# The second layer's weights split without GpSimd, and both parts of the last batch's work taken together

## The chip, the cores and the metric

The kernel runs on one core of one Trainium2 chip. The metric is the device time of one execution in microseconds (us); the time of before is a median of 3 runs. A profile records one execution, engine by engine: TensorE (PE, with its weight loads as PEld), VectorE (DVE), ScalarE (ACT), GpSimd (POOL) and SyncE (SP), whose queue issues most DMAs.

## The reference

Three layers one behind the other: an attention between 512 positions and 32 states for each of 8 batches and 8 heads, a dense layer, and a layer of 8 experts in which each token goes to one expert.

```python
scores = scale * np.matmul(x, state.transpose(0, 1, 3, 2))   # softmax, then a @ state
scores2 = scale * np.matmul(state, x.transpose(0, 1, 3, 2))  # softmax, then a2 @ x
x = np.concatenate([xread, sread], axis=2)                   # 8 x 544 tokens, 512 wide
...
h = x @ w_in                                                 # 512 -> 2048
g = np.maximum(0.01 * h, h)
x = g @ w_out                                                # 2048 -> 512
...
e_idx = np.argmax(x @ w_gate, axis=1)                        # 8 experts
for e in range(E):
    h = np.maximum(x[mask] @ w1[e], 0.0)                     # 512 -> 1024
    ye = h @ w2[e]                                           # 1024 -> 512
    out[mask] = gate_w[mask, None] * eom[mask, e, None] * ye
```

All inputs are fp32. The change is in the preparation of `w1` and `w2`, 8 experts with 4 MB together for each.

## The kernel before

PE multiplies numbers that are split in two parts, a high and a low one, with three products for each product of the reference. The dense layer uses two fp32r parts, the expert layer two fp16 parts. So the expert weights have to be split before that layer begins, and this runs beside the dense layer.

**The main loop** (from line 917) runs over steps `n`. A step is one block of 128 of the 2048 hidden columns (`f`, 0 to 15) of one chunk `c`; chunks 0 to 7 are the batches, chunk 8 holds the states' tokens. So step `n` is chunk `n // 16`, block `n % 16`. In a step, `mm1(n)` makes the hidden block `h` on PE (for two steps at a time behind a `kps` product), ACT and DVE make `u` from it (the leaky ReLU), then its parts `gh` (ACT) and `gl` (DVE), and `mm2(n - 2)`, two steps behind, adds the block before to four banks `y`. `gl` of a step is written at the start of the next one. `kl` is the low part of the other factor of `mm1`. The attention of the next batch runs beside it, up to the sixth chunk. At a chunk's end the four `y` are copied, their squares summed (ACT) and the **router** started, in pieces that `pump()` takes, one a step: split each row block in two fp16 halves (`halves`, lines 111 and 112), transpose them by DMA (`turn`, `yT`), logits on PE (`pl`, `lg`), choice, places (`pr`), scatter by POOL.

**The weight work** is the generator `presplit` (its loop from line 633), 32 jobs of two halves of 128 x 1024 fp32 each. `advance(pre)` takes it one of four parts on:

1. store the second half of the job before, load, sum the squares of the first half (ACT, `squares`, line 97);
2. the squares of the second half;
3. sum over the partitions (`tot`, two small products on PE, line 139), a power of two as scale from it (the norm: lines 647, 103, 104, 106 on DVE), then `halve` the first half;
4. store the first half, load, `halve` the second.

`halve` makes the fp16 high part `pc[:, 0]` on DVE (line 627), scales the fp32 tile in place on DVE (line 628), and subtracts on POOL for the low part (line 629). Of the 64 halves 14 belong to the last batch.

One part is taken in each step from step 14 on (line 957); in the last batch (`c` is 7, `f` from 2) a second one behind `mm2` and the pump (line 987). There parts 1 and 2 fall in even steps and 3 and 4 in odd ones, so a job takes two steps. In step 124 the states' result is split for chunk 8 (`srl`, line 933), at its start.

The order within an engine is the order in which the program is written: nothing is reordered, and an instruction that waits holds up all that stand behind it on its engine or queue.

Of the kernel before, what the change touches and what calls it, by code (L numbers as in the profile page):

```python
# [15 lines left out]
ALU = mybir.AluOpType  # L16
# [7 lines left out]
def tile_attention_moe_moe2(ctx, tc, x, state, w_in, w_out, w_gate, w_ogate, w1, w2, out):  # L24
    nc = tc.nc
    B, H, S, D = x.shape
# [54 lines left out]
                                   op=ALU.arith_shift_right)  # L81
    nc.vector.tensor_copy(tqf, tq)
    for t in range(NSR // 128):
        nc.vector.scalar_tensor_tensor(out=toks[:, t:t + 1], in0=tqf, scalar=float(TB - NS),
                                       in1=pidx_f, op0=ALU.mult, op1=ALU.add)
# [7 lines left out]
    def squares(o, t):  # L93

        k, n = t.shape[1:]
        with nc.allow_low_precision(reason="of the sum only the exponent is used"):
            nc.scalar.activation(out=junk[:, 0:k * n].rearrange("p (k n) -> p k n", n=n), in_=t, func=ACTF.Square,
                                 scale=2.0 ** 0.5, accum_out=o)
# [10 lines left out]
    def parts16(h, l, t, s):  # L109

        nc.vector.tensor_scalar(out=h, in0=t, scalar1=s, scalar2=None, op0=ALU.mult)
        nc.vector.scalar_tensor_tensor(out=l, in0=t, scalar=s, in1=h, op0=ALU.mult, op1=ALU.subtract)
# [22 lines left out]
    def over_partitions(*cols):  # L135

        ps = psa.tile([128, cols[0].shape[1]], FP32, tag="a", name="tot")
        for i, t in enumerate(cols):
            nc.tensor.matmul(ps, ones16.bitcast(BF16), t, start=(i == 0), stop=(i == len(cols) - 1))
        return ps  # L140
# [235 lines left out]
    def advance(g):  # L376
        try:
            next(g)
            return True
        except StopIteration:  # L380
            return False
# [210 lines left out]
    def presplit():  # L592

        jobs = [(e, half, m) for e in range(E) for half in range(2) for m in range(2)]

        SPARE = (NF * (B - 1) - NF + 2) // 4 + 1
        spare = {}

        def load(n, i):
            if n >= len(jobs) or (n, i) in spare:  # L600
                return spare.pop((n, i), None)
            e, half, m = jobs[n]
            k = (n - SPARE + 1) % 3 if n >= SPARE else 0
            shape = [128, KD, F2 // 4] if m == 0 else [128, KF // 4, DM]
            if k == 0:
                t = ps_p.tile(shape, FP32, tag="raw", name="raw")
            else:
                if i == 0:
                    room = x_p.tile([128, R, H, D], FP32, tag="x", name="x") if k == 1 else \
                        at1.tile([128, HP, R, 128], FP32, tag="xT", name="xT")  # L610
                    spare[n] = room.rearrange("p a b c -> p (a b c)").rearrange("p (i k f) -> p i k f", i=2, k=shape[1])
                t = spare[n][:, i]
            q = slice((2 * half + i) * 256, (2 * half + i + 1) * 256)
            if m == 0:
                nc.sync.dma_start(t, w1[e, :, q].rearrange("(k p) f -> p k f", p=128))
            else:
                nc.sync.dma_start(t, w2[e, q].rearrange("(k p) d -> p k d", p=128))
            return t

        def ahead(n):  # L620
            if n < len(jobs):
                t = load(n, 0), load(n, 1)
                spare[n, 0], spare[n, 1] = t

        def halve(t, s):
            pc = pq_p.tile([128, 2] + list(t.shape[1:]), FP16, tag="pc", name="pc")
            nc.vector.tensor_scalar(out=pc[:, 0], in0=t, scalar1=s, scalar2=None, op0=ALU.mult)
            nc.vector.tensor_scalar(out=t, in0=t, scalar1=s, scalar2=None, op0=ALU.mult)
            nc.gpsimd.tensor_tensor(out=pc[:, 1], in0=t, in1=pc[:, 0], op=ALU.subtract)  # L629
            return pc  # L630

        t0, last = load(0, 0), None
        for n, (e, half, m) in enumerate(jobs):
            wd = w1d if m == 0 else w2d
            if last is not None:
                nc.sync.dma_start(*last)
            t1 = load(n, 1)
            if n >= SPARE:
                ahead(n + 2)
            ss = sm.tile([128, 2], BF16, tag="ss2w", name="ss2w")  # L640
            squares(ss[:, 0:1], t0)
            yield
            squares(ss[:, 1:2], t1)
            yield
            sa = sm.tile([128, 1], FP32, tag="saw", name="saw")
            s = esc[:, m, half, e:e + 1]
            nc.vector.tensor_scalar(out=sa, in0=over_partitions(ss[:, 0:1], ss[:, 1:2]), scalar1=128.0, scalar2=2.0 ** -94,
                                    op0=ALU.mult, op1=ALU.max)
            norm_scale(sm, sa, s, einv[:, m, half, e:e + 1])
            pc = halve(t0, s)  # L650
            if n == SPARE - 1:
                ahead(n + 1)
                ahead(n + 2)
            yield
            nc.sync.dma_start(wd[e, :, 2 * half], pc)
            t0 = load(n + 1, 0)
            last = wd[e, :, 2 * half + 1], halve(t1, s)
            yield
        nc.sync.dma_start(*last)
# [23 lines left out]
    pre = presplit()  # L683
# [233 lines left out]
    for n in range(len(steps) + DEPTH):  # L917
        if n < len(steps):
            c, f = steps[n][0], steps[n][1]
            if f == 0:  # L920
                if attn_gen[0] is not None:
                    drain(attn_gen[0])
                    attn_gen[0] = None
                if c == 0:
                    attn_gen[0] = first_chunk()
                elif c + 1 < B:
                    attn_gen[0] = attention(c + 1)
            if c == B - 1 and f == 12:
                for i in range(2):
                    th = at.tile([128, 2, NSR], FP32R, tag=f"a1h{i}", name="srh")  # L930
                    tl = at.tile([128, 2, NSR], FP32R, tag=f"a1l{i}", name="srl")
                    nc.scalar.copy(out=th, in_=srT[:, 2 * i:2 * i + 2])
                    nc.vector.tensor_tensor(out=tl, in0=srT[:, 2 * i:2 * i + 2], in1=th.bitcast(FP32), op=ALU.subtract)
                    srh += [th[:, 0], th[:, 1]]
                    srl += [tl[:, 0], tl[:, 1]]
            if lo_part is not None:
                lo_part()
            hi_part = mm1(n)
            if c == B and f > 2:
                pump()  # L940
        conv = convert(n + 4, n + 1) if n + 1 < NF else convert()
        advance(conv)
        attend()
        if n < len(steps):
            lo_part = hi_part()
        elif lo_part is not None:
            lo_part()
            lo_part = None
        if n == 2:
            load_gates()  # L950
        if n == NF - 4:
            gate_squares()
        if n == NF - 3:
            gate_weights()
        drain(conv)
        if n + 2 >= NF:
            advance(pre)
        if n == NF * B:
            drain(pre)
            weight_scales()  # L960
            room.append([x_p.tile([128, R * H * D], FP32, tag="x", name="room"), 0])
            room.append(carve(E, E))
            nc.gpsimd.memset(room[1], 1.0)
            nc.gpsimd.affine_select(out=room[1], in_=room[1], pattern=[[1, E], [-1, E]], compare_op=ALU.is_ge,
                                    fill=0.0, base=0, channel_multiplier=0)
        if n == len(steps) - 3:
            w32_stack.close()
            wp = ctx.enter_context(tc.tile_pool(name="wp", bufs=1, side="right"))
            while active:
                pump()  # L970
            slot_regs(0)
            for q in range(4):
                w1t.append(wp.tile([128, 2, KD, F2 // 4], FP16, name=f"w1t{q}"))
                load_w(w1t, w1d, 0, q)
            for q in range(4):
                w2t.append(wp.tile([128, 2, KF // 4, DM], FP16, name=f"w2t{q}"))
                load_w(w2t, w2d, 0, q)
            for b in range(2):
                gather(b, r_p.tile([128, 2 * ROW], FP16, tag=f"row{b + 2}", name="row", bufs=1))
        if n == len(steps) + DEPTH - 1:  # L980
            transp(0, r_p.tile([128, 2 * KD, 128], FP16, tag="y", name="xt"))
        if n >= DEPTH:
            mm2(n - DEPTH)
        if n < 4:
            attend()
        pump()
        if c == B - 1 and f >= 2:
            advance(pre)
    ab.close()


# [96 lines left out]
```

## Time and profile before

| | |
|---|---|
| median of 3 runs (lowest, highest) | 1241.1 us (1239.32, 1241.99) |
| profiled execution, time | 1242.63 us |
| profiled execution, span of its trace | 1240.9 us |
| mean granted clock of PE | 0.977 of full speed |
| busy: PE, DVE, ACT, POOL | 95%, 64%, 39%, 31% of the span |
| line 629, POOL, 128 x 1024 (64 of them) | 152.00 us in all |

The busy share of an engine is an average over stages with different limits. What a change is worth has to be read in each stage from the engine that waits there and from what it waits for. Times within the trace are in us from the start of its span, which is 1.7 us shorter than the time of the execution.

### The profile page before, as it was taken

How to read it: one execution, taken by the hardware profiler on the slowest of the kernel's cores; microseconds unless marked ns; L12 is line 12 of the kernel's file. 1: busy time of each engine (PE TensorE's matmuls, PEld its weight loads, DVE VectorE, ACT ScalarE, POOL GpSimd, SP SyncE). 2: the span in 40 equal slices, each digit the busy share in tenths (PEclk: the TensorE clock that was granted, in tenths of full speed). 3: DMA queues.
4: the chain of work that ended last, by engine and by line, in shares of the span. 5: the costliest groups of instructions: out<-in, count | busy, mean ns of one | idle time of the engine just before them, and what ended most of it. 6: DMA issues, size and time to landing. Idle time of an engine off the chain costs nothing. (4 is left out here: it accounts for less than half of the span.)

```text
span 1240.9 us, 24399 instructions
## 1 busy us (share of the span) xinstructions
PE 1173.9 (95%) x9366; PEld 874.0 (70%) x9366; DVE 788.4 (64%) x1631; ACT 486.6 (39%) x950; POOL 380.4 (31%) x290
## 2 busy tenths in 40 slices
PE   5889999999999999999998887999999999999995
PEld 3557677777777777777776666877777777777773
DVE  6998786786786776786777888744643333333332
ACT  4876644544544545535444444321111111111111
POOL 3877224233323233232242353121211111111110
PEclk9899999999999999999998989999999999999998
DMA  5745346335445535445346732164216611133410
GB/s 164 223 154 136 107 119 170 99 111 170 132 119 146 154 106 165 112 129 151 95 145 187 212 135 87 52 204 166 74 52 240 260 53 44 44 128 111 182 50 23
DMA packets 133129, 161.65 MB, mean 130 GB/s; under 512 B 80015, under 2 KB 96399, under 8 KB 133008
## 3 DMA queue, kind: packets, MB, share of 16 engines
q1 hardware_dynamic: 124128, 131.65, 35.5%
q0 software_dynamic: 8880, 28.40, 6.6%
q8 instruction: 75, 1.23, 0.4%
q14 instruction: 46, 0.38, 0.1%
HBM read 229.71 MB, written 52.20 MB: 227 GB/s over the span
## 5 line engine op out<-in xcount | busy, mean ns | idle before, releaser
L739 PE MATMUL y<-woh,gh 128*128 128x512 f32 x544 | 227.7, 419 | 0.0
L741 PE MATMUL y<-woh,gl 128*128 128x512 f32 x544 | 217.3, 399 | 0.9 <-DVE gl L198 0.9
L740 PE MATMUL y<-wol,gh 128*128 128x512 f32 x544 | 217.0, 399 | 0.0
L629 POOL TENSOR_TENSOR pc<-raw,pc 128x1024 f16<-128x1024 f32 x54 | 128.0, 2370 | 248.7 <-issue 178.0
L1012 PE MATMUL h<-xt,w1t 128*128 128x128 f16 x1184 | 201.3, 220 | 0.0
L1013 PE MATMUL h<-xt,w1t 128*128 128x128 f16 x1184 | 201.2, 220 | 0.0
L1014 PE MATMUL h<-xt,w1t 128*128 128x128 f16 x1184 | 201.2, 219 | 0.0
L722 DVE TENSOR_TENSOR u<-h,u 128x512 f32<-128x512 f32 (+1 forms) x144 | 94.5, 657 | 114.7 <-ACT u L721 114.6
L1018 ACT ACTIVATE r<-h,room 128x512 f32<-128x512 f32 x74 | 50.8, 687 | 258.0 <-PE h L1014 258.0
L1020 DVE TENSOR_SCALAR rh<-h,room 128x512 f16<-128x512 f32 x74 | 55.5, 750 | 125.4 <-ACT r L1018 125.3
L1047 POOL DMA_INDIRECT out_dram<-osb,ti x37 | 37.5, 1014 | 310.9 <-DVE ti L1045 301.7
L197 ACT CAST gh<-u 128x512 fp32r<-128x512 f32 (+1 forms) x144 | 85.5, 594 | 109.0 <-DVE u L722 108.8
L739 PEld LDWEIGHTS y<-woh,gh 128*128 128x128 f32 x544 | 105.1, 193 | 31.9 <-issue 12.7
L741 PEld LDWEIGHTS y<-woh,gl 128*128 128x128 f32 x544 | 104.8, 193 | 25.6 <-DVE gl L198 1.3
L1012 PEld LDWEIGHTS <-w1t 128*128 128x128 f16 x1184 | 116.2, 98 | 4.7 <-issue 0.5
L1013 PEld LDWEIGHTS <-w1t 128*128 128x128 f16 x1184 | 116.2, 98 | 4.1
L740 PEld LDWEIGHTS y<-wol,gh 128*128 128x128 f32 x544 | 105.4, 194 | 18.8
L721 ACT ACTIVATE u<-h 128x512 f32<-128x512 f32 (+1 forms) x144 | 82.3, 572 | 88.4 <-PE h L717 86.9
L198 DVE TENSOR_TENSOR gl<-u,gh 128x512 fp32r<-128x512 f32 (+1 forms) x144 | 108.6, 754 | 12.1 <-ACT gh L197 10.3
L1014 PEld LDWEIGHTS <-w1t 128*128 128x128 f16 x1184 | 116.2, 98 | 0.0
L1037 PE MATMUL o<-w2t,rl 128*128 128x512 f16 x296 | 112.2, 379 | 0.1
L1035 PE MATMUL o<-w2t,rh 128*128 128x512 f16 x296 | 112.2, 379 | 0.1
(221 smaller groups left out, 2216.6 us busy)
## 6 DMA issues: line engine op xcount, KB each, us to landing
w1t<-w1s SPq DMA_DIRECT2D x152, 512.0 KB
w2t<-w2s SPq DMA_DIRECT2D x152, 512.0 KB
raw<-in_moe_w_dram SPq DMA_DIRECT2D x54, 512.0 KB
w1s<-pc SPq DMA_DIRECT2D x32, 512.0 KB
w2s<-pc SPq DMA_DIRECT2D x32, 512.0 KB
x<-in_x_dram SPq DMA_DIRECT2D x32, 256.0 KB
wir<-in_moe_w_in_dram SPq DMA_DIRECT2D x16, 512.0 KB
wor<-in_moe_w_out_dram SPq DMA_DIRECT2D x16, 512.0 KB
```

What stands on the lines that cost most here:

```text
L197: nc.scalar.copy(out=h, in_=t)
L198: return lambda: nc.vector.tensor_tensor(out=l, in0=t, in1=h.bitcast(FP32), op=ALU.subtract)
L629: nc.gpsimd.tensor_tensor(out=pc[:, 1], in0=t, in1=pc[:, 0], op=ALU.subtract)
L722: nc.vector.tensor_tensor(out=u, in0=ps, in1=u, op=ALU.max)
L739: nc.tensor.matmul(ys[c][t], gh[:, sl], woh[f], start=(f == 0), stop=False)
L740: nc.tensor.matmul(ys[c][t], gh[:, sl], wol[f], start=False, stop=False)
L741: nc.tensor.matmul(ys[c][t], gl[:, sl], woh[f], start=False, stop=(f == NF - 1))
L1012: nc.tensor.matmul(ps[:, i, :], wh, xt[:, k, :], start=(k == 0), stop=False)
L1013: nc.tensor.matmul(ps[:, i, :], wh, xt[:, KD + k, :], start=False, stop=False)
L1014: nc.tensor.matmul(ps[:, i, :], wl, xt[:, k, :], start=False, stop=(k == KD - 1))
L1035: nc.tensor.matmul(ps, h, w2t[q][:, 0, fi, :], start=(f == 0), stop=False)
L1037: nc.tensor.matmul(ps, l, w2t[q][:, 0, fi, :], start=False, stop=(f == KF - 1))
```

## The change

`halve` now calls `parts16`, which the router uses already. The high part is made as before; the low part is made by one DVE instruction (line 112) that scales the fp32 tile, subtracts the high part and writes fp16. The tile is no longer scaled in place, and POOL has no part in it. In the last batch the second `advance(pre)` stands directly behind the first, ahead of `mm2` and the pump.

```diff
         def halve(t, s):
             pc = pq_p.tile([128, 2] + list(t.shape[1:]), FP16, tag="pc", name="pc")
-            nc.vector.tensor_scalar(out=pc[:, 0], in0=t, scalar1=s, scalar2=None, op0=ALU.mult)
-            nc.vector.tensor_scalar(out=t, in0=t, scalar1=s, scalar2=None, op0=ALU.mult)
-            nc.gpsimd.tensor_tensor(out=pc[:, 1], in0=t, in1=pc[:, 0], op=ALU.subtract)
+            parts16(pc[:, 0], pc[:, 1], t, s)
             return pc
...
         if n + 2 >= NF:
             advance(pre)
+            if c == B - 1 and f >= 2:
+                advance(pre)
...
         pump()
-        if c == B - 1 and f >= 2:
-            advance(pre)
```

The function that it calls (line 109 on):

```python
def parts16(h, l, t, s):
    nc.vector.tensor_scalar(out=h, in0=t, scalar1=s, scalar2=None, op0=ALU.mult)
    nc.vector.scalar_tensor_tensor(out=l, in0=t, scalar=s, in1=h, op0=ALU.mult, op1=ALU.subtract)
```

In the new kernel lines 629 to 954 have numbers lower by 2; the function above keeps its own. PE's instructions stand in the same order in both kernels. On the others the order shows the following.

DVE in the last batch, steps 117 and 118, before and then changed (`xT` is the buffer from which this job's halves are read, `lg` the router's logits, `saw` and `esc` the norm):

```order
L106 TENSOR_SCALAR einv<-u 128x1
L627 TENSOR_SCALAR pc<-xT,esc 128x1024
L628 TENSOR_SCALAR xT<-xT,esc 128x1024
L524 COPY lg<-pl 128x16
L627 TENSOR_SCALAR pc<-xT,esc 128x1024
L628 TENSOR_SCALAR xT<-xT,esc 128x1024
L198 TENSOR_TENSOR gl<-u,gh 128x512
L722 TENSOR_TENSOR u<-h,u 128x512
```

```order
L106 TENSOR_SCALAR einv<-u 128x1
L111 TENSOR_SCALAR pc<-xT,esc 128x1024
L112 SCALAR_TENSOR_TENSOR pc<-xT,esc,pc 128x1024
L111 TENSOR_SCALAR pc<-xT,esc 128x1024
L112 SCALAR_TENSOR_TENSOR pc<-xT,esc,pc 128x1024
L524 COPY lg<-pl 128x16
L198 TENSOR_TENSOR gl<-u,gh 128x512
L720 TENSOR_TENSOR u<-h,u 128x512
```

The second half has moved ahead of the copy of the logits; the number of instructions is the same, and `gl` and `u` of the next step stand behind both halves in both kernels. The same happens in step 115 with a row block of the router and in step 119 with a copy of logits.

ACT in steps 120 and 121, before and then changed (`ss2w` holds the squares' sums, `dd` and `z` are the router's):

```order
L197 CAST gh<-u 128x512
L97 ACTIVATE junk,ss2w<-x 128x1024
L551 ACTIVATE dd<-dd 128x32
L562 ACTIVATE z<-z 128x4
L97 ACTIVATE junk,ss2w<-x 128x1024
L721 ACTIVATE u<-h 128x512
```

```order
L197 CAST gh<-u 128x512
L97 ACTIVATE junk,ss2w<-x 128x1024 x2
L551 ACTIVATE dd<-dd 128x32
L562 ACTIVATE z<-z 128x4
L719 ACTIVATE u<-h 128x512
```

The second square has moved ahead of the two small Exps. It is the only place where ACT's order changes.

SP's queue in steps 115 to 117, before and then changed (`w1s` and `w2s` are the split weights in DRAM):

```order
L514 DMA_TRANSPOSE yT<-row 128x8x128
L655 DMA w2s<-pc 128x2048
L636 DMA w2s<-pc 128x2048
L615 DMA x<-in_moe_w_dram 128x4x256 x2
L514 DMA_TRANSPOSE yT<-row 128x8x128 x2
L655 DMA w1s<-pc 128x2048
```

```order
L653 DMA w2s<-pc 128x2048
L514 DMA_TRANSPOSE yT<-row 128x8x128
L634 DMA w2s<-pc 128x2048
L615 DMA x<-in_moe_w_dram 128x4x256 x2
L514 DMA_TRANSPOSE yT<-row 128x8x128
L653 DMA w1s<-pc 128x2048
L514 DMA_TRANSPOSE yT<-row 128x8x128
```

In two places a transposition of the router now stands behind the store of a first half.

## Rows read from the trace of the kernel before

**Rows 1.** The page, part 1: busy time of each engine (share of span, instructions).

```profile
PE 1173.9 (95%) x9366; PEld 874.0 (70%) x9366; DVE 788.4 (64%) x1631; ACT 486.6 (39%) x950; POOL 380.4 (31%) x290
```

**Rows 2.** Waits of PE, 480 to 640 us: total, times, longest, in us.

```profile
PE tot L139 <- DVE u L722: 1.5, 2, 0.8
```

**Rows 3.** Groups of DVE, 125 to 640 us: busy, mean ns, idle before, releaser.

```profile
L722 DVE TENSOR_TENSOR u<-h,u 128x512 f32<-128x512 f32 x94 | 64.6, 688 | 95.8 <-ACT u L721 95.7
```

**Rows 4.** Waits of PE, 640 to 830 us, columns as in 2.

```profile
PE tot L139 <- ACT junk L97: 12.3, 8, 4.1
...
PE h L717 <- DVE kl L194: 2.3, 1, 2.3
```

**Rows 5.** DVE in order of time, 680 to 760 us: start, duration, idle before.

```profile
683.23 0.69 DVE L722 TENSOR_TENSOR u<-h,u 128x512 f32<-128x512 f32 x1 [0.52 <-ACT u L721]
...
687.34 0.69 DVE L722 TENSOR_TENSOR u<-h,u 128x512 f32<-128x512 f32 x1 [0.94 <-ACT u L721]
...
701.32 2.61 DVE L627 TENSOR_SCALAR pc<-raw,esc 128x1024 f16<-128x1024 f32 x1
...
705.23 0.69 DVE L722 TENSOR_TENSOR u<-h,u 128x512 f32<-128x512 f32 x1
...
711.23 0.69 DVE L722 TENSOR_TENSOR u<-h,u 128x512 f32<-128x512 f32 x1 [1.19 <-ACT u L721]
...
718.53 0.69 DVE L722 TENSOR_TENSOR u<-h,u 128x512 f32<-128x512 f32 x1 [0.73 <-ACT u L721]
...
723.53 0.68 DVE L722 TENSOR_TENSOR u<-h,u 128x512 f32<-128x512 f32 x1
...
724.75 0.75 DVE L627 TENSOR_SCALAR pc<-xT,esc 128x1024 f16<-128x1024 f32 x1
...
726.21 0.75 DVE L627 TENSOR_SCALAR pc<-xT,esc 128x1024 f16<-128x1024 f32 x1
726.99 2.52 DVE L628 TENSOR_SCALAR xT<-xT,esc 128x1024 f32<-128x1024 f32 x1
729.43 3.68 DVE L933 TENSOR_TENSOR srl<-srT,srh 128x512 fp32r<-128x512 f32 x2
733.04 0.68 DVE L198 TENSOR_TENSOR gl<-u,gh 128x512 fp32r<-128x512 f32 x1
733.64 0.68 DVE L722 TENSOR_TENSOR u<-h,u 128x512 f32<-128x512 f32 x1
...
744.24 0.68 DVE L722 TENSOR_TENSOR u<-h,u 128x512 f32<-128x512 f32 x1
...
754.98 3.25 DVE L194 TENSOR_TENSOR kl<-w,kh 128x512 fp32r<-128x512 f32 x2
```

**Rows 6.** POOL in order of time, 720 to 760 us, columns as in 5.

```profile
726.43 2.53 POOL L629 TENSOR_TENSOR pc<-xT,pc 128x1024 f16<-128x1024 f32 x1 [1.94 <-issue]
...
730.39 2.17 POOL L629 TENSOR_TENSOR pc<-xT,pc 128x1024 f16<-128x1024 f32 x1
```

**Rows 7.** Lines 627, 628 and 112: durations, minimum, median, maximum in ns.

```profile
L627 DVE TENSOR_SCALAR pc<-raw,esc x54: 695/753/2606, 132.9 to 740.4; 128x1024 f16<-128x1024 f32 x54
...
L628 DVE TENSOR_SCALAR raw<-raw,esc x54: 752/753/2529, 133.6 to 741.2; 128x1024 f32<-128x1024 f32 x54
...
L112 DVE SCALAR_TENSOR_TENSOR row<-y,s,row x34: 750/752/2508, 143.4 to 824.2; 128x512 f16<-128x512 f32 x34
```

**Rows 8.** Groups of DVE, whole span, columns as in 3.

```profile
L722 DVE TENSOR_TENSOR u<-h,u 128x256 f32<-128x256 f32 x16 | 6.7, 417 | 2.7 <-ACT u L721 2.7
```

**Rows 9.** ACT in order of time, 700 to 715 us, columns as in 5.

```profile
709.58 1.04 ACT L97 ACTIVATE junk<-x 128x1024 bf16<-128x1024 f32 x1
```

**Rows 10.** PE in order of time, 695 to 705 us, columns as in 5.

```profile
697.86 0.16 PE L139 MATMUL tot<-ss2w,ones 128*128 128x1 bf16 x1 [0.56 <-ACT junk L97]
```

**Rows 11.** Windows of 10 us: busy us (instructions), PEclk, DMA share, GB/s.

```profile
750.00:760.00 10.00, 7.67 (x42) 6.72 (x42) 9.86 (x17) 2.48 (x6) 6.43 (x8) 0.92 0.27 107
760.00:770.00 10.00, 9.09 (x48) 7.56 (x47) 5.04 (x13) 5.28 (x15) 0.00 (x0) 0.91 0.00 0
```

## The prediction

> **What bounds the kernel now.** I read the page first: TensorE (PE) is busy for 95% of the span [rows 1]. Waits of PE are therefore what a change off PE can win, and they have to be looked for stage by stage. In the middle, from 480 to 640 us, the only wait of PE's own is 1.5 us in two pieces [rows 2]. VectorE (DVE) has air there: before 94 `u` instructions it stood idle for 95.8 us, waiting for ScalarE's `u`, which waits for PE [rows 3]. So in the middle PE sets the pace. From 640 us, where the last batch takes two parts of the weight work per step, this turns round: PE waits 12.3 us for `tot`, the small sum over partitions, in 8 pieces, and 2.3 us for `kl` [rows 4].
>
> Why `tot` is late can be followed along DVE [rows 5]. I call a round the time from `u` of one even step to `u` of the next even one; one block of weights, two halves, goes through in it. In a round each thing waits for the one before: `u`, ACT's cast, two squares, `tot` on PE, DVE's norm, first half, second half, `gl`, and the next `u`. The rounds end at 683.23, then (two rounds on) 705.23, 718.53, 733.64 and 744.24 us. The round from 718.53 took 15.1 us. In it one instruction of line 628, plain 0.75 us work, took 2.52 us, and two of line 933 took 3.68 us together where the shorter row of such a 512 wide instruction (`gl`, 733.04) is 0.68 us. Under each lies a subtraction on GpSimd (POOL): one from 726.43 to 728.96 us and one from 730.39 to 732.56 us [rows 6], and the DVE instruction ends some 0.5 us behind it. The medians of lines 627 and 628 are 0.753 us and their longest 2.606 and 2.529 us [rows 7]: two lengths, one with a subtraction in the way and one without.
>
> The Trainium skill's GPSIMD Engine Reference, section Key points, says that GpSimd shares its SBUF interfaces with VectorE and contends with instructions that read two tensors from SBUF or run in a two-port mode. The trace agrees: line 628 has one tensor and takes as long for 1024 elements as line 112 for 512 [rows 7], line 933 has two tensors, and both show the long times.
>
> **The change, part by part.** *The subtraction on POOL goes* (64 of them), and with it these stalls. In the last batch that is a matter of DVE's order alone, since POOL's result is waited for only by the store.
>
> *One DVE instruction takes the place of another.* Line 628 (0.753 us [rows 7]) becomes line 112 at 1024 elements, which the trace does not have. At 512 elements line 112 takes 0.752 us [rows 7]. Bounds: no gain on what it replaces, 0.753 us, as the low one, and twice the 512 wide row, 1.504 us, as the high one. A fixed part makes twice too much: `u` of 256 elements takes 0.417 us [rows 8] and of 512 elements 0.688 us [rows 3], so 512 more cost 0.54 us. I take 0.752 + 0.54 = 1.29 us, 0.53 us more than now for each half.
>
> A rule speaks against this edit. The Trainium skill's VectorE: DVE Perf Modes, section The perf-mode tier table, has an operation on two fp32 tensors in SBUF at half the rate of one with a single tensor (2293 against 1227 ns for 2048 elements), and line 112 reads two. The rows agree: 512 elements of line 112 cost what 1024 of line 627 do. By the page's figure an estimate for 1024 elements is 1.15 us, which would shorten each round of the sum by some 0.3 us.
>
> In the middle the 0.53 us of the 50 halves ahead of the last batch, 26 us, comes out of the 95.8 us that DVE idles in front of `u` [rows 3], less what the stalls give back there. I count 0 for the time. With no such cover it would be 26 us.
>
> *The second part moves ahead of mm2 and the pump.* On PE nothing changes its place. On ACT, once, the second square comes before two small Exps: 1.04 us [rows 9] that the `u` behind them no longer waits for. On DVE a row split or a copy of logits goes behind the second half, three times. On SP two transposes go behind the store of the first half, which now waits for DVE and no longer for POOL. I count 0: each has over a step until PE needs it.
>
> **The sum**, round by round along DVE, in times of the profile [rows 5]. Pieces: from `u` to the next step's `u`, by 683.23 and 687.34, 4.1 us; from that to the first half, 723.53 to 724.75, 1.22 us; a half now is 1.46 us (724.75 to 726.21) and becomes 1.99 us; `gl` 0.60 us (733.04 to 733.64). A plain round is 4.1 + 1.22 + 3.98 + 0.60 = 9.9 us.
> - To `u` at 705.23: one wait of PE, 0.56 us [rows 10], goes, and one stall of 1.86 us (line 627 at 701.32, 2.61 less 0.75) against 1.06 us for two dearer halves: 0.8 us. Together 1.3 us, so 703.9. The like stall a round earlier made the 0.56 us and is in it.
> - To 718.53: the step between took 6.00 us (705.23 to 711.23), because the router's chain lies in it. That chain follows PE and gains only the 0.56 us, and the 1.04 us of the square go: 711.23 − 0.56 − 1.04 = 709.6. Then 1.22 + 3.98 + 0.60 = 5.8: 715.4, 3.1 us earlier. PE's wait there is gone.
> - To 733.64: 4.1 + 5.8 and twice 0.60 us for line 933 without its stall, 11.1 in place of 15.1 us: 726.5, 7.1 us earlier.
> - To 744.24: a plain round, 9.9 in place of 10.6 us: 736.4, 7.8 us earlier.
> - To `kl`: 4.1 + 5.8 and 0.68 us for `kl` itself, 10.6 us: 747.0. Now `kl` begins at 754.98 us and the first of the two comes out some 2.6 us later, at 757.6. So PE goes on 10.6 us earlier, if it is there. Its own work since that round's `tot` needs about as long, so I take 10.1 us.
> - The clock: at 750 to 770 us two windows of 10 us have 0.92 and 0.91 of full speed [rows 11]. With half speed as the other level that is 3.4 us at 1.2 GHz behind the `kl` wait, which lose 1.7 us. Without that wait they stay at 2.4 GHz: 1.7 us.
>
> Sum: 10.1 + 1.7 = 11.8 us. From the profiled execution's 1242.63 us this leaves 1230.8 us. That execution lies 1.5 us above the median of the runs shown, 1241.1 us; from the median I predict 1229.3 us. The first of the 8 waits for `tot` I leave as it is: its chain runs over the squares of `y` on ACT, behind the batch before.
>
> Bounds: with 1.504 us for the new instruction each of the last four rounds is 0.43 us longer: 10.1 us saved, 1231.0 us. With 0.753 us DVE's rounds are shorter than PE's own work, and PE's work limits the gain; I allow 3 us more. The clock may fall once more or once less: 1.7 us either way.
>
> **Rivals.**
> - *The stalls aren't POOL's work.* Then the long instructions stay long, and each of the last six rounds has 1.06 us more DVE work: 6.4 us, less the 1.04 us of the square, 5.4 us slower, 1246.5 us. This decides if line 112 or 933 still shows 2.5 us. Against it: each stall ends with a subtraction. 5%.
> - *Transposes late.* Two of them now wait for the first half's store. Should PE wait for one as long as it waits for `tot` at the longest, 4.1 us [rows 4], with 1.7 us of clock behind it, half the gain goes: 1235.1 us. For it: SP's order is fixed. Against it: they are issued steps ahead of their use. 14%.
> - *The gain is given back*: PE comes earlier to the last rows of the router and to the gathers, whose waits grow: 1241 us. Against it: these chains start from PE's own last product of the batch. 5%.
> - *More goes than I count*, for a new instruction near 0.75 us or a first wait that shrinks: 1224 us. 4%.
>
> **How the numbers follow.** My forecast, 1225.5 to 1233 us, has 72%. With 1225 to 1236 us I take in the bounds and the late transposes. A measurement of this kernel tells about 0.2%, 2.5 us, from no change. Faster: 72 + 14 + 4 = 90%. Same: 5%. Slower: 5%.
>
> **What the changed profile would show.** Right: no group on POOL with `pc`; 64 instructions of line 112 with 1024 elements at about 1.29 us and no 2.5 us ones among lines 111, 112 and 933 in the last batch; `u` to `u` near 10 to 11 us there; the waits for `tot` down from 12.3 to about 7 us, most of it the first one; no wait for `kl`. In the middle PE's waits stay as they are, with less idle time before `u`. The prediction is wrong if `tot` still waits for 12 us, if the new instruction is above 1.5 us, or if PE waits for `yT` in the last batch's first half.

## The result and the profile after

The changed kernel takes 1228.27 us in the median of 4 runs (1226.08 to 1229.55), the kernel before, run beside it, 1240.21 us (4 runs, 1239.13 to 1241.99): 11.9 us less, a ratio of 0.9898 with an interval of 0.9879 to 0.9917. A second set of runs beside the kernel before on another chip gave 0.9913 (0.9891 to 0.9936). Both medians of the changed kernel, 1228.3 and 1230.1 us, lie in the predicted range.

The first part of the page, after, answers to [rows 1]. POOL has lost 64 instructions and 156 us; PE's share has not moved, since its work is the same and the span is shorter:

```profile
PE 1165.5 (95%) x9366; PEld 867.5 (71%) x9366; DVE 775.9 (63%) x1631; ACT 488.1 (40%) x950; POOL 223.9 (18%) x226
```

Durations of line 112 after (minimum, median, maximum in ns), to be held against [rows 7]. The new instruction takes 1.283 to 1.285 us, up to 1.955 us in the form with `raw` (six of them over 1.4 us, each begun 0.45 us behind the start of line 334 on POOL, an instruction that the change does not touch); the 512 wide ones of the router, which went up to 2.508 us, now end at 0.753 us:

```profile
L112 DVE SCALAR_TENSOR_TENSOR pc<-raw,esc,pc x54: 1283/1285/1955, 132.5 to 731.3; 128x1024 f16<-128x1024 f32 x54
L112 DVE SCALAR_TENSOR_TENSOR row<-y,s,row x34: 750/752/753, 142.8 to 807.9; 128x512 f16<-128x512 f32 x34
L112 DVE SCALAR_TENSOR_TENSOR pc<-x,esc,pc x6: 1283/1283/1285, 675.4 to 742.2; 128x1024 f16<-128x1024 f32 x6
```

Waits of PE after, 640 to 830 us (total, times, longest), which answer to [rows 4]. The wait for `kl` is gone, `tot` has 8.9 in place of 12.3 us, and its longest piece is 2.4 in place of 4.1 us:

```profile
PE tot L139 <- ACT junk L97: 8.9, 7, 2.4
PE pl L522 <- DMA yT<-row: 3.2, 1, 3.2
PE t L888 <- DMA row<-srt,room: 1.0, 1, 1.0
PE y L739 <- DVE gl L198: 1.0, 1, 1.0
```

DVE after in order of time (start, duration, idle before), the places of [rows 5]:

```profile
680.37 0.68 DVE L720 TENSOR_TENSOR u<-h,u 128x512 f32<-128x512 f32 x1
...
700.95 0.68 DVE L720 TENSOR_TENSOR u<-h,u 128x512 f32<-128x512 f32 x1
...
712.20 0.68 DVE L720 TENSOR_TENSOR u<-h,u 128x512 f32<-128x512 f32 x1
...
716.29 0.69 DVE L720 TENSOR_TENSOR u<-h,u 128x512 f32<-128x512 f32 x1 [0.28 <-ACT u L719]
...
720.23 1.28 DVE L112 SCALAR_TENSOR_TENSOR pc<-xT,esc,pc 128x1024 f16<-128x1024 f32 x1
721.44 1.29 DVE L931 TENSOR_TENSOR srl<-srT,srh 128x512 fp32r<-128x512 f32 x2
722.64 0.68 DVE L198 TENSOR_TENSOR gl<-u,gh 128x512 fp32r<-128x512 f32 x1
723.24 0.68 DVE L720 TENSOR_TENSOR u<-h,u 128x512 f32<-128x512 f32 x1
...
732.49 1.80 DVE L198 TENSOR_TENSOR gl<-u,gh 128x512 fp32r<-128x512 f32 x1
734.21 0.68 DVE L720 TENSOR_TENSOR u<-h,u 128x512 f32<-128x512 f32 x1
...
744.04 1.32 DVE L194 TENSOR_TENSOR kl<-w,kh 128x512 fp32r<-128x512 f32 x2
```

The reader sees the pair of line 931 (933 before) at 1.29 in place of 3.68 us, the pair `kl` at 1.32 in place of 3.25 us, and one long instruction left, `gl` at 732.49, beside a subtraction of another line on POOL that the change does not touch (`kl`, line 194, 732.12 to 733.74 us).

In the middle nothing moves for PE: 1.5 us of waits in two pieces again, as [rows 2]. But the group that answers to [rows 3] has not less idle time, as was forecast, but a little more:

```profile
L720 DVE TENSOR_TENSOR u<-h,u 128x512 f32<-128x512 f32 x94 | 64.8, 689 | 98.0 <-ACT u L719 98.0
```

### The profile page after: what moved, and what is told of

The parts are those of the page before. It is cut to its first block, busy times and chain, and to the rows that moved or that the text cites. A ratio compares the mean times of both kernels' runs of the same rounds, so it can differ in the third digit from the quotient of the medians.

```text
span 1224.4 us, 24273 instructions
## 1 busy us (share of the span) xinstructions
PE 1165.5 (95%) x9366; PEld 867.5 (71%) x9366; DVE 775.9 (63%) x1631; ACT 488.1 (40%) x950; POOL 223.9 (18%) x226
## 5 line engine op out<-in xcount | busy, mean ns | idle before, releaser
L737 PE MATMUL y<-woh,gh 128*128 128x512 f32 x544 | 224.3, 412 | 0.0
L739 PE MATMUL y<-woh,gl 128*128 128x512 f32 x544 | 214.4, 394 | 1.0 <-DVE gl L198 1.0
L738 PE MATMUL y<-wol,gh 128*128 128x512 f32 x544 | 213.9, 393 | 0.0
L198 DVE TENSOR_TENSOR gl<-u,gh 128x512 fp32r<-128x512 f32 (+1 forms) x144 | 107.3, 745 | 12.1 <-ACT gh L197 10.3
L1033 PE MATMUL o<-w2t,rh 128*128 128x512 f16 x296 | 112.2, 379 | 0.1
L1034 PE MATMUL o<-w2t,rh 128*128 128x512 f16 x296 | 112.2, 379 | 0.0
L713 PE MATMUL h<-a1h,kh 128*128 128x512 f32 x256 | 109.5, 428 | 0.0
```

The source lines that it names most:

```text
L198: return lambda: nc.vector.tensor_tensor(out=l, in0=t, in1=h.bitcast(FP32), op=ALU.subtract)
L713: nc.tensor.matmul(ps, k_h[gi][:, k, sl], mh[k], start=(k == 0), stop=False)
L737: nc.tensor.matmul(ys[c][t], gh[:, sl], woh[f], start=(f == 0), stop=False)
L738: nc.tensor.matmul(ys[c][t], gh[:, sl], wol[f], start=False, stop=False)
L739: nc.tensor.matmul(ys[c][t], gl[:, sl], woh[f], start=False, stop=(f == NF - 1))
L1033: nc.tensor.matmul(ps, h, w2t[q][:, 0, fi, :], start=(f == 0), stop=False)
```

## The experiments

Ratios are to the kernel before, run on the same chip in turn with the experiment. The first four kernels ran on a chip where the kernel before takes 1252.43 us; where their expectations give a time, its distance to the kernel before counts. What is longer on that chip lies behind the first `kl`: from there to the end the four profiled executions take 494 to 496 us, all others 479 to 483 us.

### Which part of the change gains

The halves alone, with the second part at its old place, and the move alone, with the old halves:

```diff
-            if c == B - 1 and f >= 2:
-                advance(pre)
...
         pump()
+        if c == B - 1 and f >= 2:
+            advance(pre)
```

> The first half of the change alone: halve calls parts16, the second advance of the last batch stays behind mm2 and the pump. Theory A (the gain comes from the subtraction on POOL, which held up DVE in the last batch's rounds): nearly the whole gain, less the 1.04 us of the one square that stands behind two Exps again: 1228 to 1231 us. Rival B (the gain comes from taking both parts together): near before, 1238 to 1241 us. Rival C (half of each): 1233 to 1236 us.

> The second half of the change alone: the second advance directly behind the first, halve as before with the subtraction on POOL. Theory A: the stalls stay, only the 1.04 us of the square go: 1237 to 1241 us, with DVE instructions of 2.5 us in the last batch. Rival B: 1228 to 1231 us. Rival C: 1233 to 1236 us.

Measured: the halves alone 1245.51 against 1252.43 us, 0.9939 (0.9920 to 0.9958); the move alone 1253.30 us, 1.0008 (0.9994 to 1.0022). The gain comes from the new halves, and the move by itself shows none in the time. The 6.9 us of the halves alone lie in rival C's range (some 5 to 8 us less), below theory A's (10 to 13); on the second chip, below, the same kernel gains 10.0 us. With the old halves the stalls stay in either order: in the run of the move alone 7 of the 18 instructions of line 628 between 640 and 760 us take 2.5 us, with 0.75 us as the plain length [rows 7]. Its trace has 70.6 us from `u` of step 116 to the first `kl`, 74.4 before, so the order may be worth something there; why nothing of it is left in the time stays open.

The changed kernel and the halves alone were then run beside one another:

> The changed kernel once more, beside the kernel before on the chip of these runs; the other runs are set against this one. Theory (the halves gain by themselves, the second part's new place adds the square that no longer delays u, about 1 us, and a few waits that follow from it): 0.985 to 0.993 of the kernel before, 9 to 18 us less, and 1 to 5 us less than the halves alone. Rival (the new place is worth nothing, as when it was moved with the old halves): the same as the halves alone within 1.5 us.

> The new halves with the second part at its old place, behind mm2 and the pump. Theory: 1 to 5 us above the changed kernel, and the u behind the last router's two Exps late by about 1 us again, since the second square stands behind them. Rival: equal to the changed kernel within 1.5 us, the difference seen so far being one of chips.

Measured against 1241.70 us: changed 1230.09 us, 0.9913; halves alone 1231.75 us, 0.9922 (0.9906 to 0.9939). The medians differ by 1.7 us, but the intervals overlap, so the times alone do not tell them apart. The traces do: from `u` of step 116 to the first `kl` the changed kernel takes 64.4 us (682.43 to 746.8), the halves alone 66.3 us (682.20 to 748.5). 1.04 us of that is the one step in which the square stood ahead of the Exps (6.54 against 5.50 us, the amount forecast), another 0.9 us a step later, where DVE waits 1.18 us for the router's `pr`. That is one execution of each.

### Where it gains

Old halves for the 50 ahead of the last batch, new ones for its 14 (`SPARE` is the job with which they begin), with the second part at its new place:

```diff
+            if n < SPARE:
+                nc.vector.tensor_scalar(out=pc[:, 0], in0=t, scalar1=s, scalar2=None, op0=ALU.mult)
+                nc.vector.tensor_scalar(out=t, in0=t, scalar1=s, scalar2=None, op0=ALU.mult)
+                nc.gpsimd.tensor_tensor(out=pc[:, 1], in0=t, in1=pc[:, 0], op=ALU.subtract)
+            else:
+                parts16(pc[:, 0], pc[:, 1], t, s)
```

> The changed kernel, but the first 50 halves (those ahead of the last batch) are split as before, with the subtraction on POOL; the last 14 as changed. Theory A (only the last batch's rounds are worth time, PE covers the rest): as the changed kernel, 1226 to 1231 us. Rival D (the middle wins too, since stalls go there as well): 1231 to 1239 us, by as much as the middle is worth.

Measured: 1245.01 us, 0.9939 (0.9916 to 0.9961). The whole change did not run on this chip; its ratios elsewhere, 0.9898 and 0.9913, are 3 to 5 us lower, with intervals that touch this one. By its distance to the kernel before, 7.4 us, it lies in rival D's range (some 2 to 10 us less) and not in theory A's (10 to 15). But the halves alone, with all 64 new, gained no more on this chip (0.9939), so its times don't show that the first 50 are worth anything. The traces say how little it can be in the middle: from `u` of step 48 to `u` of step 112 this run takes 352.0 us, the kernel before 351.7, the changed kernel and the halves alone 351.5. So the gain seen here is that of the last 14 halves.

Next the new instruction a second time, into a scratch tile that nobody reads, in one run in the last 14 halves (as below), in the other in the first 50 (`n < SPARE`):

```diff
             parts16(pc[:, 0], pc[:, 1], t, s)
+            if n >= SPARE:
+                nc.vector.scalar_tensor_tensor(out=scratch(t), in0=t, scalar=s, in1=pc[:, 0], op0=ALU.mult, op1=ALU.subtract)
```

> The changed kernel with the new instruction (1.285 us) done a second time, into a scratch tile that nobody reads, in each of the last batch's 14 halves. Theory (there DVE's chain sets the pace, each round holds two halves): 2 x 1.29 = 2.6 us more in each of the last five or six rounds, less what PE's own work hides of it, 11 to 16 us above the changed kernel, so that the gain is gone; the waits for tot grow to 20 us or more, and the wait for kl comes back. Rival (PE sets the pace there too once the stalls are gone): under 4 us.

Measured: 1244.71 us, 14.6 us above the changed kernel beside it, 1.0023 of before (1.0008 to 1.0038). There DVE's chain sets the pace, and what is added to it is paid: from `u` of step 116 to the first `kl`, where 12 of the 14 halves lie, it takes 77.5 us against 64.4. The waits for `tot` grew to 13.0 us and not to 20: PE waits more often at other places of the chain too, and `kl` is back (640 to 830 us):

```profile
PE tot L139 <- ACT junk L97: 13.0, 11, 2.5
PE pl L522 <- DMA yT<-row: 3.2, 1, 3.2
PE t L895 <- DMA row<-srt,room: 2.2, 1, 2.2
PE h L722 <- DVE kl L194: 1.9, 1, 1.9
```

> The changed kernel with the new instruction (1.285 us) done a second time, into a scratch tile that nobody reads, in the 50 halves ahead of the last batch: 64 us more of VectorE. Theory (there PE sets the pace, and VectorE has 98 us of idle time in front of u): as the changed kernel within 3 us, 8 to 13 us below the kernel before; the idle time in front of u falls from 98 to about 35 to 45 us, and PE's waits from 120 to 640 us grow by no more than 3 us. Rival (the idle time lies at the wrong places, so that a half of 3.3 us holds up the u behind it): 10 us or more above the changed kernel.

Measured: 1252.37 against 1238.81 us, 1.0107 (1.0087 to 1.0126), 13.6 us above the kernel before, where the changed kernel is 11 to 12 us below it. **The theory missed here, the rival held.** DVE's groups of the middle, 125 to 640 us, in this run:

```profile
L727 DVE TENSOR_TENSOR u<-h,u 128x512 f32<-128x512 f32 x90 | 61.9, 688 | 61.5 <-ACT u L726 61.5
...
L634 DVE SCALAR_TENSOR_TENSOR scr<-raw,esc,pc 128x1024 f16<-128x1024 f32 x45 | 57.5, 1278 | 0.0
```

The idle time in front of `u` fell by 36.5 us in this window, which now holds four steps fewer, and 57.5 us of work came in: the rest is paid by PE, whose waits from 100 to 640 us now include `h` for `u` (6.2 us) and two waits of the attention (4.4 and 2.7 us). From `u` of step 48 to `u` of step 112 it takes 364.2 us, 12.7 us more than the changed kernel, and the last batch's way from `u` of step 116 to `kl` is as long as there (64.4 us). Idle time that a group shows in sum is no store to draw from. The new waits fit the rival's reason, that the longer half does not fit into the step that it falls in, whatever is left in the next.

### What a stall is

The subtraction goes back to POOL beside the new instruction, into a scratch tile:

```diff
             parts16(pc[:, 0], pc[:, 1], t, s)
+            nc.gpsimd.tensor_tensor(out=scratch(t), in0=t, in1=pc[:, 0], op=ALU.subtract)
```

> The changed kernel, and POOL does its old subtraction besides, into a scratch tile that nothing reads: DVE has the same work as in the changed kernel, no result of POOL's is waited for, and only the work beside DVE is back. Theory A: the stalls return on top of the dearer DVE instruction, so slower than before: 1241 to 1250 us, with DVE instructions of 2.5 us or more. Rival E (POOL's result or its queue made the difference, not the contention): as the changed kernel, 1226 to 1231 us.

Measured: 1307.38 us, 1.0443 (1.0417 to 1.0468), far more than the theory of contention had. DVE and POOL in order of time show why:

```profile
584.34 1.28 DVE L112 SCALAR_TENSOR_TENSOR pc<-raw,esc,pc 128x1024 f16<-128x1024 f32 x1
584.44 3.19 POOL L633 TENSOR_TENSOR scr<-raw,pc 128x1024 f16<-128x1024 f32 x1 [5.10 <-issue]
585.54 2.64 DVE L198 TENSOR_TENSOR gl<-u,gh 128x512 fp32r<-128x512 f32 x1
```

The scratch subtraction needs only the high part, so it begins under line 112, which runs on in its 1.28 us; `gl`, which begins while POOL works, ends 0.55 us behind POOL. This happens to 35 of the 128 `gl`: their mean is 1309 ns, against 785 ns in the changed kernel, 67 us more in sum. In the kernel before, the subtraction of such a half began 0.23 us after `gl` had (574.13 and 573.90 us), and `gl` took 0.68 us. So the same edit was run with the subtraction held back behind line 112, by reading the low part:

```diff
-                                    in1=pc[:, 0], op=ALU.subtract)
+                                    in1=pc[:, 1], op=ALU.subtract)
```

> As the run with the subtraction back on GpSimd into a scratch tile, with the same kinds of operands, but it now reads the low part instead of the high one, so that it can begin only behind the new VectorE instruction and not under it. Theory (a VectorE instruction with all its operands in SBUF is held until GpSimd's end if it begins while the subtraction runs, and not if it began before): gl begins about 0.2 us ahead of the subtraction and keeps its 0.69 us; of the 66 us above the changed kernel's place most goes, the ratio to the kernel before falls from 1.044 to between 0.995 and 1.015, the mean of gl from 1.31 to under 0.85 us; what is left are long instructions among the second halves of the last batch. Rival (every VectorE instruction beside a subtraction is slowed in proportion to the time they share): gl stays above 1.1 us and the ratio above 1.03.

Measured: 1254.22 against 1240.28 us, 1.0106 (1.0086 to 1.0125), `gl` at 779 ns on average, inside the forecast. The same instructions on the same engines, one begun 0.2 us behind `gl` instead of 1.1 us ahead of it, and 34 of the 44 thousandths are gone. DVE and POOL in order of time:

```profile
579.44 1.28 DVE L112 SCALAR_TENSOR_TENSOR pc<-raw,esc,pc 128x1024 f16<-128x1024 f32 x1
580.65 0.68 DVE L198 TENSOR_TENSOR gl<-u,gh 128x512 fp32r<-128x512 f32 x1
580.87 2.48 POOL L633 TENSOR_TENSOR scr<-raw,pc 128x1024 f16<-128x1024 f32 x1 [10.91 <-DVE pc L112]
581.83 0.69 DVE L726 TENSOR_TENSOR u<-h,u 128x512 f32<-128x512 f32 x1 [0.50 <-ACT u L725]
582.44 0.68 DVE L250 COPY xT<-bank 128x512 f32<-128x512 f32 x1
583.03 0.86 DVE L111 TENSOR_SCALAR pc<-raw,esc 128x1024 f16<-128x1024 f32 x1
```

`u` and the copy begin under the subtraction and keep their time; both read what PE wrote (`h`, `bank`). Line 111, all in SBUF, begins 0.32 us ahead of POOL's end (583.35) and ends 0.54 us behind it. In the last batch the second half stands directly behind the first, and there, from 714 to 765 us, five instructions of line 112 take 3.04 to 3.06 us. From `u` of step 116 to the first `kl` the run takes 77.3 us, 12.9 us of the some 24 us by which it stays above the changed kernel.

### The waits that were left

In the last batch's even steps the two squares stand ahead of ACT's cast `gh`, once with the new halves and once with the old ones. The run with the old halves has the move too: in odd steps the second part stands directly behind the first.

```diff
+        early = c == B - 1 and f >= 2 and f % 2 == 0
+        if early:
+            advance(pre)
+            advance(pre)
         if n < len(steps):
             lo_part = hi_part()
...
-        if n + 2 >= NF:
+        if n + 2 >= NF and not early:
```

> The changed kernel, but in the last batch's even steps the two squares stand ahead of ACT's cast gh, so that they don't wait for DVE's u. Theory (what is left of the waits for tot, 8.9 us in 7 pieces, comes from the squares standing behind u and gh): each piece of about 1 us goes, 4 to 7 us less than the changed kernel. Rival: gh, 2 us later, holds up DVE's gl and so the halves, and the next step's u on ACT; the rounds stay as long or grow: the same or up to 5 us more than the changed kernel.

> The old halves, with GpSimd's subtraction, and the squares of the last batch's even steps ahead of ACT's cast gh. Theory (the squares' place costs about 1.1 us a round whatever the halves are, and the stalls stay): 4 to 8 us less than the kernel before, with 2.5 us instructions still among the halves in the last batch, and 10 us or more above the run with the new halves and the squares first. Rival (the squares' place matters only once the stalls are gone): the same as the kernel before within 3 us.

Measured: with the new halves 1220.63 us, 9.5 us below the changed kernel that ran beside it, 0.9825 of before (0.9806 to 0.9845). This is the fastest kernel of the study, and its gain is larger than the theory had. With the old halves 1231.66 against 1238.81 us, 0.9945 (0.9925 to 0.9965), 7.2 us less, inside the forecast, with long instructions still there (line 628 2.53 us at 689.37). So the squares' place costs either way, and the stalls on top of it; how much of the 7.2 us belongs to the move, which by itself showed no gain in the time, is not told apart. Waits of PE with the new halves, 640 to 840 us:

```profile
PE pl L522 <- DMA yT<-row: 2.9, 1, 2.9
PE t L888 <- DMA row<-srt,room: 2.1, 1, 2.1
PE y L739 <- DVE gl L198: 1.0, 1, 1.0
PE tot L139 <- ACT junk L97: 0.9, 1, 0.9
PE h L715 <- DVE kl L194: 0.2, 1, 0.2
```

Six of the seven pieces of `tot` are gone. From `u` of step 116 to the first `kl` it takes 56.7 us (681.10 to 737.8) against 64.4, and 1.3 us more are won ahead of it. The theory counted the waits that it saw; the rounds became shorter than that: the first two together 17.6 us in place of 20.6, the one behind line 933 7.9 in place of 11.0, where the `gl` that POOL holds has also slipped off the chain to PE's next `tot`.

## Why the prediction was right

**The sum.** From `u` of step 116 on, the rounds came out as worked out. The profiled execution after is 2.86 us ahead at that `u` (680.37 against 683.23 us); with this added back, its times stand beside those of the sum:

| end of | before | predicted | after, plus 2.86 |
|---|---|---|---|
| two rounds, `u` | 705.23 | 703.9 | 703.8 |
| round with the router, `u` | 718.53 | 715.4 | 715.1 |
| round with line 933, `u` | 733.64 | 726.5 | 726.1 |
| next round, `u` | 744.24 | 736.4 | 737.1 |
| first `kl` on DVE | 757.6 | 747.0 | 747.6 |
| PE's first product with it | 757.6 | 747.5 | 747.9 |

So 10.0 us were saved along DVE, of 10.6 forecast; the second profile of the changed kernel gives 10.0 too (683.23 to 757.6 us is 74.4, 682.43 to 746.8 is 64.4). A count beside it: in this stretch ten DVE instructions were 17.8 us longer than their plain lengths before and one is 1.1 us longer after, and twelve halves are dearer by 0.53 us each, 10.3 us in all. PE went on 9.7 us earlier in the first profile and 8.1 in the second, of 10.1 forecast; in the second `kl` was out 1.9 us before PE came to it. The new instruction's 1.285 us is the estimate of 1.29 us, which was two rows added: a 512 wide instruction and the price of 512 more elements. The estimate from the Trainium skill's VectorE: DVE Perf Modes, section The perf-mode tier table, 1.15 us, was low by 0.13 us; the measurement decides.

**One round was mis-sized.** For the round to 744.24 a plain 9.9 us was forecast; 11.0 us was measured (723.24 to 734.21). 1.1 us of it is the `gl` at 732.49, held by POOL's own `kl` of line 194, which the sum had left out. In the table it shows as 0.7 us only, because the rounds ahead were 0.4 us shorter together than forecast.

**The waits for `tot`** fell to 8.9 us where about 7 was forecast, and the split was wrong: not most of it in the first, but 2.4 us there (2.7 before; the longest before, 4.1 us, is the one at 736.08 us) and six pieces of 1.0 to 1.3 us. The prediction took that chain, `u`, `gh`, two squares, `tot`, as a fixed part of the round (4.1 us from `u` to the next step's `u`) and did not see PE waiting at its end, as it does after in four of the six rounds; the run with the squares first shows its place to be worth 9.5 us.

**The clock's term** had sign and place right. Behind the wait for `kl` the kernel before runs at the lower of the two levels from 758.5 to 761.9 us; after, the same products, from 745.07 us on, run at the upper one, and the windows from 740 to 760 us stand at 1.00. The first row is before, the second after; the distance from one such product to the next is 0.43 and 0.23 us:

```profile
759.82 0.63 PE L740 MATMUL y<-wol,gh 128*128 128x512 f32 x1
746.51 0.40 PE L738 MATMUL y<-wol,gh 128*128 128x512 f32 x1
```

In the windows that answer to [rows 11] 0.92 and 0.91 have become 1.00 and 0.66, but other work stands there, since it comes some 13 us earlier:

```profile
750.00:760.00 10.00, 6.54 (x42) 5.46 (x40) 7.07 (x17) 5.80 (x16) 0.00 (x0) 1.00 0.17 34
760.00:770.00 10.00, 9.25 (x80) 7.85 (x81) 4.32 (x16) 1.71 (x4) 0.00 (x0) 0.66 0.41 74
```

The 0.66 stands behind PE's wait for `pl`, which ended at 774.86 us before, with a clock of 0.83 from 770 to 780 us, and at 760.75 us after; again before, then after:

```profile
774.86 0.26 PE L522 MATMUL pl<-gwh,yT 128*128 128x16 f16 x4 [3.19 <-DMA yT<-row]
760.75 0.28 PE L522 MATMUL pl<-gwh,yT 128*128 128x16 f16 x4 [3.25 <-DMA yT<-row]
```

Half speed went elsewhere too: at 670 to 680 us from 0.66 to 1.00, at 730 to 740 us from 0.72 to 1.00. Summed over the windows from 660 to 830 us the clock lacked 13.6 us of full speed before, 3.4 after and 5.1 in the second profile. What of this the waits covered is not told apart.

**What the sum did not have.** From PE's first product with `kl` to the end the two profiles of the changed kernel gain 3.9 and 4.0 us, where 1.7 was forecast; 1.9 and 0.9 us of it is the wait `t` for gathers, 2.9 us before. Ahead of step 116 they gain 2.9 and 0.8 us. 1.3 us gained and 0.4 us lost of that stand already at `u` of step 112 and are taken as scatter between executions: the second instruction of the very first half already lies 1.1 us apart (133.6 and 132.5 us). The rest, 1.6 and 1.2 us, falls between steps 112 and 116. There line 112 at 678.15 us took 2.51 us before and takes 0.75 after, and the clock rose; the runs do not tell the two apart. So the profiled executions gained 16.5 and 12.9 us, and that the medians' 11.9 and 11.6 us come so near to the forecast 11.8 is in part luck: PE's side of the chain gave less than forecast and the ends gave more.

**The middle** costs nothing, as counted, but not because idle time pays. On DVE, 125 to 640 us, the halves rose from 76.2 us (38.7 and 37.5, 46 each) to 99.3 (64.4 and 34.9, 47 each); line 112 of the router fell from 28.6 to 18.0 us, and the tiny line 544 (128 x 4) from 13.9 to 2.1 us. Together 118.7 before and 119.4 after, and all of DVE's work there 382.1 and 381.9 us. The stalls there gave back what the dearer halves took, and the idle time stayed. The cover that the prediction named was hardly called on, and less idle time in front of `u`, which it had as a sign, did not come; with the instruction doubled, 36.5 of 57.5 us came out of it.

**The rivals.** *The stalls aren't POOL's work* falls with line 931 and `kl` at their short times. *Transposes late*: in the last batch's first half PE never waited for `yT`; the 3.2 us for `pl` lies behind `kl`, at 760 us, and was 3.2 us before. *The gain is given back*: the wait for gathers, `t`, got shorter. *More goes than I count* was not met by this change: the new instruction took 1.285 us, and the first wait for `tot` fell by 0.2 us only. The runs with the squares first are what made it shrink, to 0.9 us.

## What to carry to other kernels

Read the stall from the instruction's length, not from the wait: here a VectorE group with two lengths, 0.75 and 2.5 us, had GpSimd in the way. Starting GpSimd's work 0.2 us behind the next VectorE instruction took back 34 of 44 thousandths, but taking it away was faster still by some 24 us. Idle time in a sum of rows is not slack at each place; before counting on it, double the work there and look. And where one chain sets the pace, ask of every link of it whether it has to stand there: the link that was taken as fixed here, two squares behind a cast on ScalarE, was worth nearly as much as the change.

## What the runs showed that was not expected

In these traces a VectorE instruction with all operands in SBUF that begins while GpSimd's two-tensor subtraction runs waits for its end and then does its work: `gl` (128 x 512) ended 0.55 us behind POOL. Of a pair of line 544 (128 x 4) in the kernel before, 2.31 us together from 355.06, the second ended 0.02 us behind a subtraction that had begun at 355.20, as it did; the line's mean in the middle was 1.20 us before and is 0.22 us after. Not all such instructions were held: the reduction of line 547 and the 128 x 1 ones of lines 309 and 310, with one tensor each, began under a subtraction in the kernel before (six of each) and kept their time. Those that read PE's banks kept it too.

One that began before GpSimd, be it by 0.1 us (line 112 at 584.34), keeps its time; in the kernel before all 36 `gl` that began 0.14 to 0.23 us ahead of a subtraction did. There is an exception among the prediction's own rows: the second of the pair of line 933 began at 730.04 us, 0.36 us ahead of the record of the subtraction [rows 6], and was held to 0.56 us behind its end. POOL had a DMA of line 587 in hand until 730.39 us; what held line 933 in these 0.36 us stays open.

The Trainium skill's GPSIMD Engine Reference, section Key points, tells of contention with instructions of two SBUF tensors or in a two-port mode. The trace agrees that it exists (`gl` reads two), and shows besides that the order of the two starts decides whether it costs nothing or 2 us; line 628, with one tensor, is held like one with two. On POOL's side the subtraction took 2.38 us on average behind line 112 and 3.15 us when it began under it.
